# Attention product by two heads of both softmaxes with halves added on VectorE, and a unit stage whose order is written one instruction at a time

## The chip, the cores and the metric

The kernel runs on one core of a Trainium2 chip. The metric is the device time of one execution in microseconds (us). The core's engines each work through their own instructions in order: TensorE (PE in the profile; PEld is its loading of weights, which overlaps the matmuls), VectorE (DVE), ScalarE (ACT), GpSimd (POOL, here mostly an issuer of DMAs) and SyncE (SP, an issuer of DMAs).

## What is computed

A gated mix of two branches on the same 2048 x 1024 input, all in float32:

```python
g = sigmoid((x * gate_w).sum(-1, keepdims=True))
# branch a: linear attention, 32 heads of 32
q, k, v = split(x @ wqkv)
pq = einsum("bhsd,hdf->bhsf", q, w_phi);  pk = the same of k
phi_q = concat(softmax(pq), softmax(-pq));  phi_k = the same of pk
kv = einsum("bhsf,bhsd->bhfd", phi_k, v);  z = phi_k summed over s
o = (phi_q @ kv) / (phi_q . z + 1e-6)
a = o @ wo
# branch b: gated MLP, 3584 wide
b = (gelu(x @ w_gate) * (x @ w_up)) @ w_down
out = g * a + (1 - g) * b
```

## The kernel before

Every float32 product is made of three matmuls in `float32r`: an operand is split into a *high* part (a copy to `float32r` on ScalarE, L421) and a *low* part (operand minus high on VectorE, L424), and `PASSES` adds high-high, high-low and low-high. A weight tile so costs one ScalarE and one VectorE operation of 128x1024.

The program has three stages.

1. Keys, values, their feature maps, `kv`, `z` and the gate (L146 to L412). Query weights are folded with `w_phi` and stored in DRAM (`wq_fold`); `kv` and `z` go to DRAM as `kz`. VectorE sets `mask` and `ones` at the very start (L64 to L67, L149); `ones` feeds seven warm-up products of TensorE (L154), and `mask` makes the block-diagonal weights `bd` of the first folds.
2. The unit stage (L438 to L972): 62 *units*, each 2 of 28 column blocks of gate (`g`), up (`u`) or query (`q`) weights times half of the tokens, by Strassen's scheme (in Winograd's form). A unit is seven products of 12 matmuls (L744): `x` into bank `a`, `y` into bank `p`, `z` and `v` and so on, where the last two products of a unit stand inside the next one. `x`, `y`, `z` and `v` are the unit's weight operands, made from staged tiles by `weights` in the pools `wgu`, `tyz` and `v`. Between the products ScalarE copies one accumulating bank to another (`c<-b` L775, `c11<-a` L777, `b<-a` L779) and empties bank `p` (L757); `results` reads the finished banks, and gelu, the product with up, or the query itself goes out by DMA on GpSimd (`lm`, `q`). Bank `p` has a single buffer: the next unit's `y` product waits for L757.
3. The output stage (L975 to L1138): attention and MLP results times `wo` and `w_down`, 3024 matmuls (L1088).

Beside the units a *background* stream works on the queries. A *job* (`attention`, L838) is one block of 128 query features (4 heads) by 512 tokens, 32 jobs in all. It loads the block, transposes it 32 by 32, takes maximum and minimum, makes both softmaxes (ScalarE's exponent, with a table load), multiplies in the denominator and gate, transposes back, splits the result into `pts`, and hands TensorE an *attention product* (L906): for each of the two softmaxes three matmuls of 128x128 weights `kbs` and 512 columns, all into one bank `misc`. ScalarE copies the bank out (L909). The background also loads the second half's tokens between the jobs.

What sets the order: in the unit stage TensorE, VectorE, ScalarE and SyncE execute in the order in which the code is written (`manual_schedule`). That order comes from generators. Time is counted in *slots* of one product (t = 7n + k for product k of unit n). Each generator yields the earliest slot, the latest slot and the cost in VectorE and ScalarE time of its next piece of work; after each product, `run_slot` takes the pieces that are due and, as long as a budget of `SLOT` = 2.65 us on each of the two engines lasts, those that may run. An attention product is placed behind product 1 or 4 of a unit, at the earliest one slot after its operand `pts` was written.

Of the kernel before, what the change touches and what calls it, by code (L numbers as in the profile page):

```python
# [8 lines left out]
F32 = mybir.dt.float32  # L9
# [22 lines left out]
def tile_gated_mix(ctx: ExitStack, tc: tile.TileContext, x, xT, wkT, wqT, wv, w_phi, wo,  # L32
# [31 lines left out]
    mask = keep.tile([P, 4, 32], F32, name="mask")  # L64
    nc.vector.memset(mask, 0.0)
    for j in range(4):
        nc.vector.memset(mask[32 * j:32 * j + 32, j, :], 1.0)  # L67
# [78 lines left out]
    with tc.tile_pool(name="kw", bufs=1) as kw, tc.tile_pool(name="kp", bufs=1) as kp, \  # L146
            tc.manual_schedule(engines={PE, DVE}):
        ones = kp.tile([P, P], F32, name="ones")
# [89 lines left out]
        def finish_kv(hh, pkv):  # L238
# [10 lines left out]
            for h in range(4):  # L249
                q = h % 2  # L250
                nc.scalar.activation(kv_c[32 * h:32 * h + 32, 4 * hh:4 * hh + 4],
                                     by_head[32 * q:32 * q + 32, :, h // 2, :, q], AF.Copy)
            yield

        def finish_z(hh, s, zacc, pz):
            nc.tensor.matmul(pz, ones, zacc[:, s].rearrange("p h f -> p (h f)"), start=True, stop=True)
            z4 = pz.rearrange("p (g h f) -> p g h f", g=4, h=4)
            for h in range(4):
                q = slice(32 * h, 32 * h + 32)
                nc.scalar.activation(zb[q, 4 * hh:4 * hh + 4, s], z4[q, :, h, :], AF.Copy)  # L260
# [177 lines left out]
    with tc.tile_pool(name="xa", bufs=1) as xa, tc.tile_pool(name="fp", bufs=1) as fp, \  # L438
# [5 lines left out]
        SLOT, NEVER = 2.65, 10 ** 9  # L444
        streams, fillers, now, left = [], [], [0], [0.0, 0.0]

        def start(gen):
            streams.append([next(gen), len(streams), gen])

        def run_slot(t, extra=0.0, scalar=0.0):  # L450

            now[0] = t
            left[:] = [min(left[0], 0.0) + SLOT + extra, min(left[1], 0.0) + SLOT + extra - scalar]
            while True:
                ready = [s for s in streams if s[0][0] <= t and (s[0][1] <= t or (
                    left[0] > 0 and (left[1] > 0 or len(s[0]) < 4)))]
                if not ready:
                    break
                s = min(ready, key=lambda s: (s[0][1], s[1]))
                for i, cost in enumerate(s[0][2:]):  # L460
                    left[i] -= cost
                s[0] = next(s[2], None)
                if s[0] is None:
                    streams.remove(s)
# [3 lines left out]
        def room(n):  # L468

            return not any(held[max(0, len(held) - 4):][:max(0, n - 4 + min(4, len(held)))])  # L470

        def hold(*parts):
            held.append(True)
            return len(held) - 1, stage(*parts, pool=fp if len(held) % 4 == 0 else None)

        def hidden():
            return fp.tile([P, BLK], F32, tag="h", name="h", bufs=3)

# [15 lines left out]
        def late_sums(kc, r1, r2):  # L494
            x_load(1, kc, r1, r2)
            yield now[0] + 2, NEVER, 2.8
            for k, t in enumerate(x_sums(r1, r2)):
                nc.gpsimd.dma_start(xs_late[k][:, kc, :], t)
            yield now[0] + 2, NEVER, 0.0
# [6 lines left out]
        def second_half(t, staging):  # L506
# [7 lines left out]
            while not free[0]:  # L514
                yield now[0] + 1, NEVER, 0.0
# [3 lines left out]
            def load(n):  # L519
                i, j, _, _ = parts[n]  # L520
                nc.sync.dma_start(staging[n % 4].rearrange("p (a b) -> p a b", a=2), srcs[i][:, 2 * j:2 * j + 2, :])

            for n in range(4):
                load(n)
            for n, (i, j, last, need) in enumerate(parts):
                s = staging[n % 4].rearrange("p (a b) -> p a b", a=2)
                yield max(now[0], last), need - 2, 0.0, 1.05
# [5 lines left out]
                yield now[0], need - 1, 1.25  # L533
                low(q[1], s, q[0])
                if n + 4 < len(parts):
                    load(n + 4)
# [8 lines left out]
        right_ops = {}  # L545

        def weights(n, half, kind, m):
# [4 lines left out]
            yield t - 7, t - 6, 0.0  # L552
            while not room(2):
                yield now[0] + 1, t - 5, 0.0
            ke, e = hold((0, 1024, w[2 * m]))
            ko, o = hold((0, 1024, w[2 * m + 1] if fresh else right_sums[kind, m][0]))
            yield t - 5, t - 3, 0.0, 1.05
# [3 lines left out]
            yield now[0] + 1, t - 2, 1.25  # L561
            low(xl, e, xh)
            mine["x"] = x
            held[ke] = fresh
            yield max(now[0], t - 4), t - 2, 1.4 if fresh else 0.0, 1.05
            if fresh:
                b11, b21, b12, b22 = e[:, :BLK], e[:, BLK:], o[:, :BLK], o[:, BLK:]
                nc.vector.tensor_tensor(b22, b22, b12, OP.subtract)
                nc.vector.tensor_tensor(b12, b11, b12, OP.subtract)  # L569

# [5 lines left out]

            y = slot()
            yh, yl = flat(y)
            high(yh, o)
            if fresh:  # L580
                if half == 0:
                    nc.gpsimd.dma_start(right_sums[kind, m][0], o)
                if n:
                    yield now[0], t - 1, 1.4
                    more_sums()
            yield now[0] + 1, t, 1.25
            low(yl, o, yh)
            mine["y"] = y
            held[ko] = False
            if n == 0:  # L590
                yield now[0], t, 1.4
                more_sums()
            if not fresh:
# [580 lines left out]
```

## Time and profile before

| | us |
|---|---|
| median of 3 runs (2382.92 to 2386.14) | 2383.41 |
| the profiled execution, its own time | 2383.34 |
| its span, first to last instruction | 2381.5 |
| keys, values and gate, up to the first unit | 462.7 |
| unit stage, first unit product to first output product | 1228.3 |
| output stage, to the end of the span | 690.5 |

A row of a grouped view gives line, engine, operation, output and input tiles with partitions x elements and type, count, then busy time and mean nanoseconds of one, then the engine's idle time ahead of it and what ended it. A row of the timeline gives start, length, engine, line and count of merged instructions. A row of the waits gives who waited for whom, in total, how often, and the longest. PE matmul rows include the tail of the last matmul, which overlaps the next row's start.

### The profile page before, as it was taken

The page shows a single profiled execution, that of the slowest core. Times are in us where ns is not written, and L with a number is a line of the kernel's source. Part 1 is how long each engine was busy: PE and PEld are TensorE (multiplying, and loading weights), DVE is VectorE, ACT ScalarE, POOL GpSimd, SP SyncE. Part 2 cuts the span into 40 slices and gives each one's busy share as a digit, 9 for nine tenths or more (in the row PEclk, how much of TensorE's full clock was granted, in tenths as well). Part 3 has the DMA queues.
Part 4 walks back from the last instruction along what each step waited for, and adds up shares of the span by engine and source line. Part 5 has one row for each costly group of instructions (what it writes and reads, how often), then busy time and mean ns, then how long its engine had stood idle before and what let it go on. Part 6 is the DMA issues. An engine that isn't in the chain of part 4 may idle for free.

```text
span 2381.5 us, 28170 instructions
## 1 busy us (share of the span) xinstructions
PE 2372.2 (100%) x10689; PEld 1969.3 (83%) x10689; DVE 1746.3 (73%) x2183; ACT 991.6 (42%) x1286; POOL 142.2 (6%) x266
## 2 busy tenths in 40 slices
PE   9999999999999999999999999999999999999999
PEld 8888888788888888888888888888888888888887
DVE  7877868858777777777767676777574878777773
ACT  4323332435445444555555555555443222323221
POOL 0000000011111121110001000000000000000000
PEclk9999999999999999999999999999999999999999
DMA  5112333544444556474444444444685767978774
GB/s 179 47 47 84 98 115 100 180 174 146 179 170 149 194 199 229 171 254 140 138 133 158 142 134 133 153 138 135 240 292 182 252 223 264 327 260 316 261 267 135
DMA packets 154360, 425.10 MB, mean 179 GB/s; under 512 B 21360, under 2 KB 21360, under 8 KB 154224
## 3 DMA queue, kind: packets, MB, share of 16 engines
q1 hardware_dynamic: 127872, 336.64, 42.6%
q0 software_dynamic: 25312, 86.52, 9.4%
q8 instruction: 84, 1.38, 0.2%
q14 instruction: 52, 0.43, 0.1%
q10 hardware_dynamic: 1040, 0.13, 0.0%
HBM read 328.34 MB, written 94.90 MB: 178 GB/s over the span
## 4 chain that ended last, share of the span: by engine, by line
PE 79%; DVE 0%; ACT 0%; issue 0%; ACTq 0%; DVEq 0%
PE po L1088 29%; PE a L744 21%; PE c L744 14%; PE b L744 7%; PE p L744 7%; PE misc L906 2%; DVE x L1048 0%; ACT L872 0%; DVE x L888 0%; DVE tyz L424 0%; ACT x L872 0%; DVE st L876 0%; DVE x L879 0%; ACT tyz L421 0%; DVE v L424 0%
## 5 line engine op out<-in xcount | busy, mean ns | idle before, releaser
L200 PE MATMUL pd<-wkv,x 128*128 128x512 f32 x1536 | 361.3, 392 | 0.0
L200 PEld LDWEIGHTS pd<-wkv,x 128*128 128x128 f32 x1536 | 284.8, 188 | 58.1 <-issue 1.0
L1088 PE MATMUL po<-tw,wgu 128*128 128x512 f32 x1344 | 309.8, 389 | 0.0
L1088 PEld LDWEIGHTS po<-tw,wgu 128*128 128x128 f32 x1344 | 252.3, 188 | 52.4
L421 ACT ACTIVATE wgu<-stage 128x1024 fp32r<-128x1024 f32 x147 | 155.2, 1057 | 291.0 <-PE po L1088 225.1
L424 DVE TENSOR_TENSOR wgu<-stage,wgu 128x1024 fp32r<-128x1024 f32 x147 | 179.6, 1222 | 123.7 <-ACT wgu L421 123.5
L424 DVE TENSOR_TENSOR tyz<-stage,tyz 128x1024 fp32r<-128x1024 f32 x126 | 153.0, 1215 | 41.8 <-ACT tyz L421 41.8
L421 ACT ACTIVATE tyz<-stage 128x1024 fp32r<-128x1024 f32 x126 | 132.7, 1053 | 115.6 <-DVE stage L569 64.3
L744 PE MATMUL a<-s,tyz 128*128 128x512 f32 x744 | 179.4, 390 | 0.9 <-DVE tyz L424 0.4
L744 PE MATMUL a<-x,wgu 128*128 128x512 f32 x744 | 178.7, 389 | 0.0
L744 PE MATMUL p<-s,tyz 128*128 128x512 f32 x744 | 178.7, 389 | 0.0
L744 PE MATMUL c<-x,wgu 128*128 128x512 f32 x744 | 178.7, 389 | 0.0
L744 PE MATMUL b<-s,tyz 128*128 128x512 f32 x744 | 178.7, 389 | 0.0
L744 PE MATMUL c<-x,tyz 128*128 128x512 f32 x744 | 178.7, 389 | 0.0
L744 PE MATMUL a<-s,v 128*128 128x512 f32 x744 | 178.7, 389 | 0.0
L744 PEld LDWEIGHTS a<-s,tyz 128*128 128x128 f32 x744 | 139.4, 188 | 31.0 <-DVE tyz L424 1.3
L744 PEld LDWEIGHTS p<-s,tyz 128*128 128x128 f32 x744 | 139.6, 188 | 29.1
L744 PEld LDWEIGHTS a<-x,wgu 128*128 128x128 f32 x744 | 139.6, 188 | 29.0
L744 PEld LDWEIGHTS c<-x,tyz 128*128 128x128 f32 x744 | 139.6, 188 | 29.0
L744 PEld LDWEIGHTS c<-x,wgu 128*128 128x128 f32 x744 | 139.6, 188 | 29.0
L744 PEld LDWEIGHTS a<-s,v 128*128 128x128 f32 x744 | 139.6, 188 | 29.0
L744 PEld LDWEIGHTS b<-s,tyz 128*128 128x128 f32 x744 | 139.6, 188 | 29.0
(176 smaller groups left out, 3423.7 us busy)
## 6 DMA issues: line engine op xcount, KB each, us to landing
stage<-lm SPq DMA_DIRECT2D x98, 512.0 KB, 3.6
sr<-in_w_down SPq DMA_DIRECT2D x84, 512.0 KB, 5.8
sl<-lm SPq DMA_DIRECT2D x70, 512.0 KB, 4.5
lm<-h POOLq DMA_DIRECT2D x112, 256.0 KB, 2.5
stage<-in_w_gate SPq DMA_DIRECT2D x43, 512.0 KB, 3.9
stage<-in_w_up SPq DMA_DIRECT2D x43, 512.0 KB, 4.2
stage<-la SPq DMA_DIRECT2D x28, 512.0 KB, 4.3
tg<-stage POOLq DMA_DIRECT2D x26, 512.0 KB, 3.1
```

What stands on the lines that cost most here:

```text
L200: nc.tensor.matmul(ps[m], xb[b, kc // 4][:, a, kc % 4, t * P:(t + 1) * P], w[:, e, m * 512:(m + 1) * 512], start=kc == 0 and i == 0, stop= ...
L421: nc.scalar.activation(dst, src, AF.Copy)
L424: nc.vector.tensor_tensor(dst, src, dst_h.bitcast(F32), OP.subtract)
L744: nc.tensor.matmul(dst, w[:, h, 4 * part + kc, :], xq[:, e, kc, :], start=first and kc == 0 and i == 0, stop=kc == 3 and i == 2, skip_grou ...
L906: nc.tensor.matmul(po, kbs[:, a, s, :], pts[:, q, s, :], start=s == 0 and i == 0, stop=s == 1 and i == 2)
L1088: nc.tensor.matmul(ps[c], ls[:, a, m, c * P:(c + 1) * P], rs[:, e, m], start=opens and m == 0 and j == 0, stop=closes and m == 1 and j == 2)
```

## The change

Two things are changed together.

**The attention product.** The layout of a job becomes 2 heads x 2 softmaxes on the partitions: a block of 32 partitions holds one softmax of one head, and the tile's two halves of the free dimension hold two pairs of heads. So `load_query` loads each block twice (four DMAs of 32 partitions x 2 x 512 for one of 128x512), a signed copy on ScalarE (`sign`, plus and minus one by 32 partitions) turns the second copy negative, and one maximum does for both softmaxes. The block-diagonal weights of a pair are 64 columns wide instead of 128. Their high and low parts stand side by side in one 128x128 weight (`kbs`), so two matmuls (with `pts` high and `pts` low) do for a pair of heads what three did, with the low-low part in addition: 4 matmuls instead of 6, into two `misc` banks. The two halves of each result are then brought together: four half-height copies on ScalarE (`other` crosses partitions, `own` does not) and one addition on VectorE. `finish_kv` and `finish_z` write `kv_c` and `zb` in the new layout.

**The order.** The slots with budgets are replaced by estimated clocks of VectorE, ScalarE and TensorE. Each generator yields an engine, a length, the time from which the work can start, and a due product; `run` writes the requests one at a time by earliest start, then due, up to the estimated start of the next product. Constants stand for a product (2.73), a signal between engines, a DMA's landing (`LAND` = 5.0) and a store. Weight loads start up to nine products ahead of the unit, the bank copies and results are one sequence (`banks`), and an attention product goes behind any product whose estimated end is later than its operand. Query units stand at places 0, 5, 10 and 15 of the first half's 30 units instead of 2, 9, 16 and 23. `mask` moves to the first stage's pool, behind the new memsets.

```diff
-    mask = keep.tile([P, 4, 32], F32, name="mask")
-    nc.vector.memset(mask, 0.0)
+    pair_mask = keep.tile([P, 2, 32], F32, name="pair_mask")
+    nc.vector.memset(pair_mask, 0.0)
+    for j in range(2):
+        nc.vector.memset(pair_mask[64 * j:64 * j + 64, j, :], 1.0)
+    sign = keep.tile([P, 1], F32, name="sign")
     for j in range(4):
-        nc.vector.memset(mask[32 * j:32 * j + 32, j, :], 1.0)
+        nc.vector.memset(sign[32 * j:32 * j + 32], 1.0 - 2 * (j % 2))
...
-        SLOT, NEVER = 2.65, 10 ** 9
+        INF, PRODUCT, SIGNAL, LAND, STORE = 10.0 ** 9, 2.73, 0.12, 5.0, 4.5
...
+        def run(j, until):
             while True:
...
+                ready = []
+                for s in streams:
+                    at = max(busy.get(s[0][0], 0.0), value(s[0][2]))
+                    if at < until:
+                        ready.append((at, s[0][3], s))
+                if ready:
+                    at, due, s = min(ready, key=lambda r: r[:2])
...
+                emit(s)
...
-                mine.insert((0, 7, 12, 19)[m] if half else 7 * m + 2, (half, "q", m))
+                mine.insert((0, 7, 12, 19)[m] if half else 5 * m, (half, "q", m))
...
-            yield t - 5, t - 3, 0.0, 1.05
+            end = yield SCA, 1.1, lambda: max(landed, done(t - 9)), t - 2.2
             x = new_weight()
...
+                    yield SCA, 0.65, lambda: done(t + 1), t + 7.7
+                    nc.scalar.activation(before[2], unit_banks[n][1], AF.Copy)
...
+            product(*args, **kw)
+            ends[j] = begins[j] + PRODUCT
+            if fillers and fillers[0][0] < ends[j]:
+                fillers.pop(0)[1](ends[j] + 0.92)
...
-            nc.sync.dma_start(work[:, 4], query[half][g][j])
+            rows = query[half][g][j].rearrange("(w h f) t -> h f w t", w=2, h=2)
+            for h in range(2):
+                for s in range(2):
+                    nc.sync.dma_start(work[64 * h + 32 * s:64 * h + 32 * s + 32, 4:6], rows[h])
...
+                end = yield SCA, 1.1, landed, now[0] + SOON
+                nc.scalar.activation(e2, e2, AF.Copy, scale=sign)
...
-                nc.vector.transpose(work[:, 7], work[:, 4])
...
-                nc.vector.tensor_reduce(mm[:, 0, :], x, AX.X, OP.max)
-                nc.vector.tensor_reduce(mm[:, 1, :], x, AX.X, OP.min)
...
+                nc.vector.transpose(wide[1], wide[0])
...
+                nc.vector.tensor_reduce(mm, f, AX.X, OP.max)
...
+                for q in range(4):
+                    nc.vector.tensor_copy(k[32 * q:32 * q + 32], t[32 * (q ^ 1):32 * (q ^ 1) + 32])
...
-                        for i, (a, q) in enumerate(PASSES):
-                            nc.tensor.matmul(po, kbs[:, a, s, :], pts[:, q, s, :], start=s == 0 and i == 0,
-                                             stop=s == 1 and i == 2)
-                    h = hidden()
-                    nc.scalar.activation(h, po, AF.Copy)
...
+                po = [misc(), misc()]
+                for s in range(2):
+                    for q in range(2):
+                        nc.tensor.matmul(po[s], kbs[:, s].rearrange("p a b -> p (a b)"), pts[:, q, s, :],
+                                         start=q == 0, stop=q == 1)
...
+            for s in range(2):
+                nc.scalar.activation(other[rows[s]], po[s][rows[1 - s]], AF.Copy)
...
+            for s in range(2):
+                nc.scalar.activation(own[rows[s]], po[s][rows[s]], AF.Copy)
...
+            nc.vector.tensor_tensor(own, own, other, OP.add)
```

On VectorE, at the program's start (the rows are numbered by place in the engine's queue, with line, operation, output and input tiles and shape), before:

```order
1 L65 MEMSET mask 128x128
2 L149 MEMSET ones 128x128
3 L67 MEMSET mask 32x32 x4
4 L177 TENSOR_TENSOR bd<-phi_c,mask 128x128 x4
5 L44 TENSOR_TENSOR wkv<-early,wkv 128x512
```

And now:

```order
1 L65 MEMSET pair_mask 128x64
2 L70 MEMSET sign 32x1 x2
3 L67 MEMSET pair_mask 64x32 x2
4 L70 MEMSET sign 32x1 x2
5 L152 MEMSET mask 128x128
6 L154 MEMSET mask 32x32 x4
7 L156 MEMSET ones 128x128
8 L184 TENSOR_TENSOR bd<-phi_c,mask 128x128 x4
```

`ones`, on which TensorE's first instructions wait, was the second memset and is now the thirteenth.

On ScalarE, in the middle of the unit stage, around the copy that empties bank `p` of the first `u` unit (`x_3592<-p`, L757), before (`tyz` and `wgu` rows are highs of weights, L713 are gelus):

```order
220 L421 ACTIVATE tyz<-stage 128x1024
221 L779 ACTIVATE b<-a 128x512
222 L713 ACTIVATE x_3592<-x_3592 128x512
223 L421 ACTIVATE v<-stage 128x512
224 L757 ACTIVATE x_3592<-p 128x512
225 L775 ACTIVATE c<-b 128x512
226 L421 ACTIVATE tyz<-stage 128x1024
227 L777 ACTIVATE c_3590<-a 128x512
```

And the same place of the first `u` unit now (the copy from `p` is L830, the high is L428):

```order
235 L820 ACTIVATE b<-a 128x512
236 L428 ACTIVATE tyz<-stage 128x1024
237 L428 ACTIVATE v<-stage 128x512
238 L751 ACTIVATE x_3593<-x_3593 128x512
239 L428 ACTIVATE wgu<-stage 128x1024
240 L428 ACTIVATE tyz<-stage 128x1024
241 L830 ACTIVATE x_3593<-p 128x512
242 L809 ACTIVATE c<-b 128x512
```

The high of a later unit's `x` (row 239) and of the next unit's `z` (row 240) have moved ahead of the copy from `p`; they stood behind it, on the far side of `c<-b`.

On ScalarE, at the end of the unit stage (the last unit's bank `p`, the last copy `c<-b`, which TensorE's very last unit product needs, and the first weights of the output stage), before:

```order
1009 L421 ACTIVATE v<-stage 128x512
1010 L757 ACTIVATE x_3592<-p 128x512
1011 L807 ACTIVATE c<-b 128x512
1012 L421 ACTIVATE tyz<-stage 128x1024
1013 L421 ACTIVATE wgu<-stage 128x1024
1014 L421 ACTIVATE wl<-stage 128x1024
```

And now:

```order
1071 L751 ACTIVATE x_3593<-x_3593 128x512
1072 L830 ACTIVATE x_3593<-p 128x512
1073 L428 ACTIVATE tyz<-stage 128x1024
1074 L428 ACTIVATE wgu<-stage 128x1024
1075 L809 ACTIVATE c<-b 128x512
1076 L428 ACTIVATE wl<-stage 128x1024
```

The copy stood ahead of the two highs and stands behind them.

On TensorE, an attention product between unit products, before 6 matmuls and now 4; first before:

```order
262 L744 MATMUL a<-x_2482,wgu 128x512 x12
263 L744 MATMUL p<-s_3385,tyz 128x512 x12
264 L906 MATMUL misc<-pts,kbs 128x512 x6
265 L744 MATMUL c<-x_2287,tyz 128x512 x12
266 L744 MATMUL a<-s_3386,tyz 128x512 x12
```

And now:

```order
244 L793 MATMUL a<-s_3387,tyz 128x512 x12
245 L793 MATMUL a<-s_3389,v 128x512 x12
246 L995 MATMUL misc<-pts,kbs 128x512 x4
247 L793 MATMUL c_3591<-x_2682,wgu 128x512 x12
248 L793 MATMUL b<-s_3388,tyz 128x512 x12
```

There are 32 such places in both; the product now stands behind any of a unit's products and not only behind two of them.

More of the change, by code (lines that the diff above doesn't have):

```diff
@@ L891, in attention @@
[L891 removed]
+                end = yield VEC, 1.27, end - SIGNAL, now[0] + SOON
+                nc.vector.transpose(wide[1], wide[0])
+                more = bool(jobs) and stored.get(jobs[0], INF) < INF and not (
+                    between and now[0] >= between[0][0] - 7)
+                if more:
+                    landed = yield SYN, LAND, max(end, stored[jobs[0]]), INF
+                    load_query(*jobs[0])
+                end = yield SCA, 1.1, lambda: max(end, pts_free[0]), now[0] + SOON
```

492 lines of the change are left out of this document (272 added, 220 removed).

## The prediction

> **What bounds the kernel now.** I read the page first (busy shares, the row of the granted clock), then who made TensorE wait, then the stage that the change rewrites, then single places in order of time.
>
> ```profile
> PE 2372.2 (100%) x10689; PEld 1969.3 (83%) x10689; DVE 1746.3 (73%) x2183; ACT 991.6 (42%) x1286; POOL 142.2 (6%) x266
> PEclk9999999999999999999999999999999999999999
> ```
>
> TensorE is busy for 2372.2 of 2381.5 us and the clock is granted in full in every slice. So a shorter time needs fewer matmuls or fewer gaps between them, and of gaps there are only 9 us in all. The view of stretches gives the unit stage after its start-up and then its first half (columns: length, busy time of PE, PEld, DVE, ACT and POOL with their instructions, granted clock, DMA share, GB/s), and the view of waits names the only waits of TensorE in that stage:
>
> ```profile
> 473.00:1691.00 1218.00, 1217.58 (x5372) 1007.82 (x5371) 892.07 (x1194) 613.68 (x841) 132.17 (x244) 1.00 0.48 164
> 473.00:1070.00 597.00, 596.58 (x2633) 493.61 (x2632) 444.96 (x594) 286.74 (x395) 83.98 (x155) 1.00 0.53 186
> ```
>
> ```profile
> PE c L703 <- DVE h L651: 1.6, 1, 1.6
> PE a L744 <- DVE tyz L424: 0.4, 1, 0.4
> PE a L744 <- ACT c L777: 0.4, 1, 0.4
> ```
>
> TensorE stands still for 0.4 of 1218 us there. All three waits lie at the stage's first unit, where the order of the work is the same before and after. VectorE and ScalarE have 326 and 604 us to spare in the stage. The change can therefore win what it takes from TensorE's queue, and nothing on the other engines; it can lose whatever new waits it puts in that queue.
>
> **The term that is removed.** The timeline shows one attention product with the product behind it, and the grouped view all of them:
>
> ```profile
> 609.08 1.52 PE L906 MATMUL misc<-pts,kbs 128*128 128x512 f32 x6
> 610.44 2.88 PE L744 MATMUL c<-x,wgu 128*128 128x512 f32 x12
> 613.16 2.88 PE L744 MATMUL b<-s,tyz 128*128 128x512 f32 x12
> ```
>
> ```profile
> L906 PE MATMUL misc<-pts,kbs 128*128 128x512 f32 x192 | 48.7, 389 | 0.0
> ```
>
> A row's length counts the tail of its last matmul, which overlaps the next row, so the step from start to start is what counts: 610.44 - 609.08 = 1.36 us for six, 2.72 us for twelve, in both cases 0.2267 us a matmul. There are 192 / 6 = 32 attention products. Each goes from six matmuls to four of the same shape (128x128 weights, 512 columns), so 64 fewer: 64 x 0.2267 = **14.5 us off TensorE**. The 62 units keep their 7 products of 12 matmuls; they only stand in another sequence.
>
> **What is added elsewhere.** The nearest rows for a job's new work:
>
> ```profile
> L860 DVE STREAM_TRANSPOSE x<-x 128x512 f32<-128x512 f32 x32 | 22.6, 706 | 0.1
> L862 DVE TENSOR_REDUCE mm<-x 128x16 f32<-128x512 f32 x32 | 22.0, 686 | 1.1
> L863 DVE TENSOR_REDUCE mm<-x 128x16 f32<-128x512 f32 x32 | 21.7, 677 | 0.0
> L893 DVE STREAM_TRANSPOSE x<-x 128x1024 f32<-128x1024 f32 x32 | 39.6, 1238 | 0.0
> L880 DVE TENSOR_REDUCE st<-x 128x32 f32<-128x1024 f32 x32 | 39.1, 1220 | 1.1
> L721 DVE TENSOR_TENSOR h<-h,x 128x512 f32<-128x512 f32 x53 | 36.7, 692 | 1.8
> L406 DVE COPY g_at<-g_a 32x16 f32<-32x16 f32 x16 | 2.8, 173 | 0.2
> L909 ACT ACTIVATE h<-misc 128x512 f32<-128x512 f32 x32 | 19.2, 599 | 100.5 <-PE misc L906 100.5
> ```
>
> VectorE, per job: the first transpose is of 1024 instead of 512 (+0.53); one reduction of 1024 (1.22 by L880) replaces two of 512 (-0.14); four small copies (4 x 0.173 = 0.69, and not below 0.5, since the shortest memsets at the program's start take 0.12 each); the small operations double in width (about +0.1); the addition of the halves (+0.69). Together 1.9 us, 60 us in 32 jobs: VectorE goes from 892 to about 953 us in a stage of some 1204, 79%. ScalarE gets the signed copy (1.06, the longest of the highs of that size in the rows below) and four half-height copies for one full one; their cost by the row is 0.3 to 0.6 each, since no row shows whether half the partitions cost less; I take 0.6 by the nearest row, +1.8. That is at most 92 us, to 59%. Both lie beside TensorE, which hides them as long as no single operand comes late. Each job's one query load becomes four of 32 partitions, 512 KB instead of 256 KB, 8 MB in all; at 164 GB/s and a DMA share of 0.48 over the stage there is room. If the cover were gone, VectorE's 60 us would be the price; that is the third rival.
>
> **New waits, place by place.** The order on ScalarE in the middle of the stage shows the copy that empties bank `p` behind the highs of two weights, where it stood right behind the bank results before. TensorE's next `p` product waits for it. Its reserve, from the rows of the same work:
>
> ```profile
> 613.90 0.59 ACT L757 ACTIVATE x<-p 128x512 f32<-128x512 f32 x1
> 615.88 2.88 PE L744 MATMUL a<-x,wgu 128*128 128x512 f32 x12
> 616.08 0.58 ACT L775 ACTIVATE c<-b 128x512 f32<-128x512 f32 x1 [1.58 <-PE b L744]
> 617.96 1.04 ACT L421 ACTIVATE tyz<-stage 128x1024 fp32r<-128x1024 f32 x1
> 618.60 2.88 PE L744 MATMUL p<-s,tyz 128*128 128x512 f32 x12
> ```
>
> Before, the copy ends at 614.49 and `p` is written again at 618.60: 4.1 us in reserve. In the new order the high of `z` stands ahead of it, and that can start only when the `b` product has ended, 0.20 us behind the start of the `a` product (616.08 against 615.88). Then 1.06 for the high and 0.59 for the copy: 1.85 us, and the `p` product starts at 2.72. **0.87 us remain**, so no wait here, but the reserve is a fifth of what it was. The high of a weight (`tyz` or `wgu`) stands directly ahead of the copy in 9 of 62 units, so I count these as the places where a wait can come up, between 0 and 1 us each; I take 0.6 us in all, nearer to nothing, since the worked place still has room.
>
> At the stage's end the copy `c<-b` moves behind two highs:
>
> ```profile
> 1685.57 2.88 PE L744 MATMUL a<-s,v 128*128 128x512 f32 x12
> 1685.83 0.58 ACT L807 ACTIVATE c<-b 128x512 f32<-128x512 f32 x1 [1.46 <-PE b L744]
> 1688.29 2.88 PE L744 MATMUL c<-x,tyz 128*128 128x512 f32 x12
> 1689.03 1.06 ACT L421 ACTIVATE tyz<-stage 128x1024 fp32r<-128x1024 f32 x1 [2.62 <-DVE stage L928]
> 1690.00 1.04 ACT L421 ACTIVATE wgu<-stage 128x1024 fp32r<-128x1024 f32 x1
> ```
>
> Highs start 0.97 us apart (1690.00 - 1689.03). From 1685.83 two highs and the copy give 1685.83 + 1.94 + 0.58 = 1688.35, and the product that needs `c` would start at 1688.29. **+0.2 us** with the hand-over, once.
>
> At the program's start VectorE gets seven more memsets, and `ones` now stands behind all of them:
>
> ```profile
> 0.83 0.17 DVE L65 MEMSET mask<- 128x128 f32 x1 [0.83 <-PEq L1166]
> 0.97 0.17 DVE L149 MEMSET ones<- 128x128 f32 x1
> 1.08 0.47 DVE L67 MEMSET mask<- 32x32 f32 x4
> 1.19 3.36 PE L154 MATMUL pd<-ones 128*128 128x128 f32 x14 [1.19 <-DVE ones L149]
> 4.67 1.44 PE L190 MATMUL pg<-bd,early 128*128 128x128 f32 x8
> 6.98 0.58 ACT L43 ACTIVATE wkv<-pg 128x512 fp32r<-128x512 f32 x1
> 7.28 1.16 PE L190 MATMUL pg<-bd,early 128*128 128x128 f32 x8 [1.17 <-DMA early<-in_wkT]
> 8.19 1.64 PE L200 MATMUL pd<-wkv,x 128*128 128x512 f32 x6
> ```
>
> Eleven memsets at 0.11 to 0.14 stand between the first and `ones`: 1.3 us later, the warm-up matmuls end at about 5.9 instead of 4.6, and the first fold with them. The second fold waits for a DMA for 1.17 us anyway, so most of this is swallowed; the copy of the first fold's result can slip from 6.98 to about 7.5, and with it the product at 8.19. Between 0 and 0.5; I take **+0.3 us**.
>
> **The sum** against the profiled execution: its time was 2383.34 us (span 2381.5 and 1.8 around it), and the median of the runs is 2383.41, the same within 0.1. 2383.3 - 14.5 + 0.6 + 0.2 + 0.3 = 2369.9, say **2370 us**, 0.56% less.
>
> **The rivals.** *The waits are more and longer than worked out* (TensorE's new waits on `p` and on bank results in many units). For it: the reserves shrink, and ScalarE's and VectorE's orders are now packed. Against it: the places that I worked out have room, and the code lets an attention product into TensorE's order only behind a product that ends, by the code's clocks, after the operand is ready. If the nine places lose 1 us each, minus the 0.6 already counted, that is 2378; half of it 2374.
>
> *The query loads land late, and ScalarE stands still behind them: slower.* The signed copy waits for them in ScalarE's one queue, and the highs, the `p` copy and the bank copies behind it wait too. The issue view (KB each, median us to landing, over the unit stage):
>
> ```profile
> stage<-in_w_gate SPq DMA_DIRECT2D x39, 512.0 KB, 3.9
> x<-q SPq DMA_DIRECT2D x32, 256.0 KB, 2.7
> x<-xs SPq DMA_DIRECT2D x6, 512.0 KB, 6.0
> ```
>
> The order places the copy for a landing 5.0 us after the issue (`LAND`). Twice the bytes cost 1.2 us more (3.9 against 2.7), and three more issues at about 0.33 each add 1.0: 4.9 us, in time. By the slowest rows, 6.0 and 1.0 make 7.0, 2.0 us late. TensorE pays only what exceeds the reserve behind the copy: with 0.87 us that is 1.1 us in each job where a tight place follows. If it follows in 20 of 32 jobs, +22 us: 2392. It decides from 14.5 / 32 = 0.45 us of TensorE wait per job, that is, landings over 6.3 us at nearly every job. Against it: at the first job the reserve is larger, as `c` is wanted two products later. The Trainium skill, DMA: Bandwidth & Descriptors, section Rules for kernel authors, speaks against such a split: transfers to separate partition groups run through the same DMA engines one after the other, so one transfer over 128 partitions is to be used. By that page's fit (about 2.0 us and bytes over 436 GB/s, section Anatomy of one DMA — SWDGE (gpsimd) path, made for loads from GpSimd, so an estimate here) 512 KB in one go would land in 3.2 us and four in a row, each with its own 2.0 us, in over 9. The rows put a load of 256 KB at 2.7 us, near the page's 2.6, but no row here shows whether four loads in flight pay the fixed part four times; if they did, 4 us late less 0.9 in 20 jobs would be over 60 us, an estimate by the page alone.
>
> *VectorE becomes the bound where jobs crowd: no change.* Query units now stand at places 0, 5, 10 and 15 of the first 30 instead of 2, 9, 16 and 23, so the 16 jobs of the first half come in some 21 units. A job is about 12.4 us on VectorE: seven operations of 1024 at 1.22, three of 512 (2.07 by the rows above) and nine small ones of about 0.2. It becomes 14.3. The first half's row has 445 of 597 us; without 16 jobs at 12.4 that is 247, or 41%, for weights and results. In the 21 units, 420 us, 16 x 14.3 and 41% make 401 us. An in-order queue this full passes any delay on, and operands of TensorE stand in it. If it came out 3% longer, 12 us would build up, less about 3 us of reserve: 2370 + 9 = 2379. Against it: the code counts 1.25 us for operations that take 1.22 by the rows, and 0.72 to 0.75 for 0.69, so the real queue should run ahead of the one planned.
>
> *The change does not do what it says.* The order has 128 attention matmuls where it had 192, so it does.
>
> **How the numbers follow.** Forecast 0.70, at 2368.5 to 2372; more waits 0.16, at 2372 to 2378; a full VectorE 0.06, at 2379 (mostly within 0.2%); late loads 0.08, at 2380 to 2392. A measurement of this kernel tells 0.2%, about 4.8 us, from no change. Faster by more (below 2378.6): 0.70, nearly all of the second case and a little of the others, 0.87; within 0.2%: 0.07; slower by more (above 2388.2): 0.06. The range takes in the forecast and the second case, from 2367.8 (no new wait, 2368.8, and 1 us of the old start-up waits gone) to 2378.
>
> **What would show it.** Right: the group of `misc` matmuls with 128 entries and about 33 us, TensorE's waits in the unit stage below 2 us in all, the unit stage some 14 us shorter, the start of the unit stage within 0.5 us of where it was. Wrong: TensorE rows that wait on the copy from `p` or on `tyz`, ScalarE waiting on the query DMA, or VectorE busy near 100% for tens of microseconds in the stage's first third. A stage whose attention matmuls do not follow each other at 0.2267 us would fell the first term.

## The result and the profile after

The changed kernel takes **2370.73 us** (median of 4 runs, 2370.57 to 2371.59); the kernel before, on the same chip, takes 2384.24 us (4 runs, 2382.92 to 2386.14). The ratio is **0.9943**, with a 95% interval of 0.9926 to 0.9961: 13.5 us or 0.57% faster. The forecast was 2370.

First the busy shares of the changed kernel:

```profile
PE 2358.1 (100%) x10625; PEld 1957.5 (83%) x10625; DVE 1795.7 (76%) x2334; ACT 1078.7 (46%) x1388; POOL 142.2 (6%) x266
```

TensorE still fills the span, with 64 matmuls fewer (10625 for 10689); VectorE has 49.4 us more than before and ScalarE 87.1. The next view has the program in three stretches, start-up, unit stage and output stage (columns as in the prediction), first the kernel before, then the changed one:

```profile
0.00:462.69 462.69, 460.17 (x2263) 388.37 (x2264) 366.92 (x496) 165.83 (x219) 7.33 (x17) 1.00 0.33 104
462.69:1691.01 1228.32, 1225.86 (x5404) 1013.70 (x5403) 900.42 (x1205) 619.84 (x850) 133.79 (x247) 1.00 0.48 164
1691.01:2381.50 690.49, 686.13 (x3025) 567.22 (x3023) 478.98 (x483) 205.96 (x218) 1.08 (x2) 1.00 0.73 254
```

```profile
0.00:463.00 463.00, 459.67 (x2263) 388.15 (x2263) 367.42 (x503) 164.42 (x211) 7.33 (x17) 1.00 0.32 104
463.00:1677.86 1214.86, 1212.80 (x5340) 1001.92 (x5339) 951.70 (x1352) 708.23 (x960) 133.76 (x247) 1.00 0.51 173
1677.86:2368.80 690.94, 685.60 (x3025) 567.38 (x3023) 476.59 (x481) 206.04 (x217) 1.08 (x2) 1.00 0.74 254
```

The unit stage is 13.46 us shorter, the start-up 0.31 and the output stage 0.45 us longer; together the 12.7 us by which the spans differ (2381.5 and 2368.8). In the unit stage VectorE works 51.3 us more and ScalarE 88.4. TensorE's waits in the changed kernel, all that there are:

```profile
PE pd L161 <- DVE ones L156: 2.5, 1, 2.5
PE c L740 <- DVE h L689: 1.6, 1, 1.6
PE pg L197 <- DMA early<-in_wkT: 0.8, 1, 0.8
PE a L793 <- ACT c L813: 0.4, 1, 0.4
```

Two of them lie in the unit stage, both at its first unit, where they were before. No new wait came up. The attention product in order of time, and its group:

```profile
529.12 2.89 PE L793 MATMUL a<-s,v 128*128 128x512 f32 x12
531.84 1.10 PE L995 MATMUL misc<-pts,kbs 128*128 128x512 f32 x4
532.78 2.89 PE L793 MATMUL c<-x,wgu 128*128 128x512 f32 x12
```

```profile
L995 PE MATMUL misc<-pts,kbs 128*128 128x512 f32 x128 | 35.2, 397 | 0.0
```

From start to start the four take 532.78 - 531.84 = 0.94 us, where four times 0.2267 is 0.907. With the old step of 1.36, 32 x (1.36 - 0.94) = 13.44 us. Added up over all 32 places the steps take 43.5 us before and 30.2 now, 13.3 less: all but 0.2 us of the unit stage's gain. (The wait of 0.4 us on `tyz` at the first unit is gone as well; the stage's end, next, takes 0.16 of it back.) The stage's end, on TensorE and then on ScalarE:

```profile
1672.26 2.88 PE L793 MATMUL a<-s,v 128*128 128x512 f32 x12
1675.01 3.02 PE L793 MATMUL c<-x,tyz 128*128 128x512 f32 x12
1677.86 11.04 PE L1190 MATMUL po<-tyz,wgu 128*128 128x512 f32 x48
```

```profile
1672.45 1.06 ACT L428 ACTIVATE tyz<-stage 128x1024 fp32r<-128x1024 f32 x1 [1.40 <-PE b L793]
1673.42 1.05 ACT L428 ACTIVATE wgu<-stage 128x1024 fp32r<-128x1024 f32 x1
1674.37 0.58 ACT L809 ACTIVATE c<-b 128x512 f32<-128x512 f32 x1
```

The copy `c<-b` stands behind the two highs as foreseen and ends at 1674.95; the `c` product starts at 1675.01. The last two products take 5.60 us instead of 2 x 2.72: +0.16.

The new work on VectorE and ScalarE, and the issue view of the query loads (KB each, median us to landing):

```profile
L963 DVE COPY st<-st 32x32 f32<-32x32 f32 x128 | 22.1, 173 | 2.4
L1015 DVE TENSOR_TENSOR h<-h,other 128x512 f32<-128x512 f32 x32 | 21.9, 686 | 5.0 <-ACT h L1012 4.9
L1006 ACT ACTIVATE other<-misc 64x512 f32<-64x512 f32 x64 | 38.1, 595 | 43.8 <-PE misc L995 43.1
L924 ACT ACTIVATE x<-x,sign 128x1024 f32<-128x1024 f32 x32 | 36.7, 1148 | 18.2 <-DMA x<-q 11.5 <-DMA kz<-kz 4.2 <-DMA stage<-in_w_up 2.3
x<-q SPq DMA_DIRECT2D x128, 128.0 KB, 2.7
```

### The profile page after: what moved, and what is told of

Its sections match the earlier page's. It is cut to its first block, busy times and chain, and to the rows that moved or that the text cites. A ratio compares the mean times of both kernels' runs of the same rounds, so it can differ in the third digit from the quotient of the medians.

```text
span 2368.8 us, 28503 instructions
## 1 busy us (share of the span) xinstructions
PE 2358.1 (100%) x10625; PEld 1957.5 (83%) x10625; DVE 1795.7 (76%) x2334; ACT 1078.7 (46%) x1388; POOL 142.2 (6%) x266
## 3 DMA queue, kind: packets, MB, share of 16 engines
q8 instruction: 83, 1.36, 0.2%
## 4 chain that ended last, share of the span: by engine, by line
PE 88%; issue 9%; DVE 1%; DMA 1%; ACT 0%; POOL 0%; SPq 0%; POOLq 0%; ACTq 0%
PE po L1190 29%; PE a L793 21%; PE c L793 14%; PE pd L207 7%; PE b L793 7%; PE p L793 7%; PE misc L995 1%; PE pg L241 1%; PE pd L197 0%; DMA raw<-in_xT 0%; PE pg L197 0%; DMA early<-in_wkT 0%; POOL wq L293 0%; DMA stage<-in_wqT 0%; DVE x L1150 0%
## 5 line engine op out<-in xcount | busy, mean ns | idle before, releaser
L428 ACT ACTIVATE wgu<-stage 128x1024 fp32r<-128x1024 f32 x147 | 155.8, 1060 | 295.6 <-PE po L1190 224.3
L793 PEld LDWEIGHTS a<-s,tyz 128*128 128x128 f32 x744 | 139.5, 188 | 30.2 <-ACT c L813 0.8
L428 ACT ACTIVATE tyz<-stage 128x1024 fp32r<-128x1024 f32 x126 | 132.9, 1055 | 54.2 <-PE c L793 18.1
```

The source lines that it names most:

```text
L428: nc.scalar.activation(dst, src, AF.Copy)
L793: nc.tensor.matmul(dst, w[:, h, 4 * part + kc, :], xq[:, e, kc, :], start=first and kc == 0 and i == 0, stop=kc == 3 and i == 2, skip_grou ...
```

## The experiments

All diffs are against the changed kernel unless the text says otherwise. Where the text says "one run", there is a single time, and a difference of a microsecond between two such times shows little.

### Six matmuls in the new order

```diff
-                    for q in range(2):
+                    for i, q in enumerate((0, 1, 1)):
                         nc.tensor.matmul(po[s], kbs[:, s].rearrange("p a b -> p (a b)"), pts[:, q, s, :],
-                                         start=q == 0, stop=q == 1)
+                                         start=i == 0, stop=i == 2)
```

> The changed kernel in its new order, but each attention product again with six matmuls (the second p-stack is multiplied twice, so the attention output is not the reference's). Theory (the gain is the 64 matmuls taken off TensorE's queue, the new order by itself is worth nothing): unit stage longer by 64 x 0.2267 = 14.5 us than in the changed kernel, about 2385 us, within 0.2% of the time before; attention steps 1.36 to 1.40 us. Rival (part of the gain comes from the new order): below 2379 us with a unit stage well under 1228 us. Second rival (the added work on VectorE and ScalarE costs time that the missing matmuls hid): above 2388 us.

Measured: 2384.95 us (median of 10) against 2383.28 of the kernel before (13 runs on the same chip), a ratio of 1.0006, 0.9996 to 1.0015. The theory holds: with the matmuls put back the whole gain is gone, and neither the new order nor the 51 and 88 us of added work gains or costs anything that this measurement can tell. The attention step here:

```profile
531.38 1.56 PE L995 MATMUL misc<-pts,kbs 128*128 128x512 f32 x6
532.78 2.89 PE L793 MATMUL c<-x,wgu 128*128 128x512 f32 x12
```

1.40 us for six where the kernel before took 1.36: the 0.04 us of slowing per attention product is there with six matmuls as with four.

### The new product in the old order

The kernel before with the new layout, product and `joined` addition as a stream of its own; slots, budgets and the order's rules as before:

```diff
-                run_slot(7 * n + k, 1.0 if fill else 0.0, 0.6 * (moved + fill))
+                run_slot(7 * n + k, 0.9 if fill else 0.0, 0.6 * (moved + 4 * fill))
...
+        def joined(own, other, half, g, j):
+            yield now[0] + 2, now[0] + 3, 0.7
+            nc.vector.tensor_tensor(own, own, other, OP.add)
+            spill(own, left_att[half], j, g)
```

> The new attention product (two heads by two softmaxes, four matmuls, VectorE adds the halves) inside the old slot-by-slot order of the unit stage, with the query units at their old places. Theory (count of matmuls alone): unit stage shorter by about 13.5 us than before, 2370 to 2373 us. Rival (the new work fits beside TensorE only in an order written instruction by instruction): new TensorE waits on bank copies, p or results of together over 4 us, 2375 us or more.

Measured: 2477.01 us (median of 4), a ratio of 1.0392, 1.0375 to 1.0409. The theory falls, and the time is on the rival's side, far beyond its number. Its mechanism, waits on bank copies and results, is only a small part of it: the one such wait of note takes 4.1 us, on the copy from `p`. TensorE's largest wait, and the last attention products in order of time:

```profile
PE misc L921 <- ACT pts L428: 83.9, 5, 17.6
```

```profile
1697.34 0.79 PE L921 MATMUL misc<-pts,kbs 128*128 128x512 f32 x1 [13.71 <-ACT pts L428]
1717.86 0.80 PE L921 MATMUL misc<-pts,kbs 128*128 128x512 f32 x1 [17.61 <-ACT pts L428]
```

The slots give a job only what the weights and results leave. With 1.6 us more per job the jobs fall behind, and five of the 32 are left when the last product of the stage has run. They then go one after the other with TensorE standing still, about 20.5 us each (1717.86 - 1697.34). The waits are hardly spread over the stage; this is a backlog paid at the end.

### Old order, with room for the jobs

The kernel of the run before this one with two edits:

```diff
-        SLOT, NEVER = 2.65, 10 ** 9
+        SLOT, NEVER = 2.96, 10 ** 9
...
-                mine.insert((0, 7, 12, 19)[m] if half else 7 * m + 2, (half, "q", m))
+                mine.insert((0, 7, 12, 19)[m] if half else 5 * m + 1, (half, "q", m))
```

At these places the four query units stand between a gate unit and its up unit and write over a kept gate result, so four pairs of the MLP come out of other numbers; the instructions are the same in number and size.

> The new attention product in the old slot-by-slot order as in e2_product_old_order, with the query units of the first half moved ahead (places 1, 6, 11, 16 instead of 2, 9, 16, 23) and 2.96 instead of 2.65 us of VectorE and ScalarE work let into a slot, so that by the code all 32 attention products stand ahead of the stage's last product. Theory (what the old order lacked in e2 was room for the jobs, so five were left over behind the last product; TensorE's count decides once they fit): attention steps of 0.91 us, unit stage 1214 to 1220 us, 2369 to 2377 us. Rival (slots that are fuller than TensorE's 2.72 us make TensorE wait for weights and banks in many units; an order written instruction by instruction is needed): unit stage over 1225 us, 2381 us or more.

Measured: 2383.94 us (median of 10) against 2384.12, a ratio of 1.000, 0.999 to 1.001. The backlog is gone, but so is the gain; the time lies just over the rival's bound. The two largest waits of TensorE in its unit stage:

```profile
PE b L751 <- ACT b L786: 5.5, 1, 5.5
PE a L751 <- DVE tyz L431: 2.5, 3, 1.6
```

These two make 8.0 us, and what runs behind a wait is slower as well (below). So in slots that can be filled this far the product's gain is given back in waits. Its attention matmuls, though, take the old 389 ns in the mean, not 397, with the same two banks and the same four matmuls:

```profile
L921 PE MATMUL misc<-pts,kbs 128*128 128x512 f32 x128 | 34.2, 389 | 0.0
```

### The start-up

```diff
+        ones = kp.tile([P, P], F32, name="ones")
+        nc.vector.memset(ones, 1.0)
...
-    nc.vector.memset(pair_mask, 0.0)
```

(the memsets of `pair_mask` and `sign` follow once the start-up's own are done.)

> The changed kernel with the memset of the ones tile put first on VectorE and the memsets of pair_mask and sign moved behind the start-up. Theory (the later start of the unit stage, 463.00 instead of 462.69 us, comes from the later warm-up matmuls): unit stage starts at 462.6 to 462.8 us, time 0.2 to 0.4 us less than the changed kernel. Rival (it comes from something else in the start-up): start stays at 463.0 us.

Measured, one run: 2371.32 us, and the warm-up matmuls did start early:

```profile
1.05 3.35 PE L156 MATMUL pd<-ones 128*128 128x128 f32 x14 [1.05 <-DVE ones L147]
```

The first row of the unit stage in this run, and then the warm-up and the first row of the unit stage in the run with the new product in the old order, whose memsets stand as in the changed kernel:

```profile
463.03 2.88 PE L793 MATMUL a<-x,wgu 128*128 128x512 f32 x12
```

```profile
2.49 3.34 PE L161 MATMUL pd<-ones 128*128 128x128 f32 x14 [2.49 <-DVE ones L156]
462.34 2.88 PE L751 MATMUL a<-x,wgu 128*128 128x512 f32 x12
```

The theory falls: with an early warm-up the stage starts late, with a late one early. Over the runs of this study whose start-up is the changed kernel's own, the stage starts between 462.33 us (three reductions more on VectorE, below) and 463.30 (eight loads, below); what decides within this microsecond was not settled.

### One bank for the four matmuls

```diff
-                po = [misc(), misc()]
+                po = [misc()] * 2
...
-                                         start=q == 0, stop=q == 1)
+                                         start=s == 0 and q == 0, stop=s == 1 and q == 1)
```

> The changed kernel with all four attention matmuls of a job accumulated into one bank instead of two into each of two banks (the halves of two softmax pairs are added up where they should stand apart, so the output is not the reference's). In the changed kernel four matmuls take 0.94 us from start to start of the products around them, 0.033 us more than 4 x 0.2267. Theory A (the extra comes from the second bank, its start and its signal): the step falls to 0.907 us and the unit stage is 1.0 us shorter. Theory B (it comes from the operands, the waits or the signals of the matmuls themselves): the step stays at 0.94 us.

Measured, one run: 2371.87 us; the row of the attention matmuls' group is the same as the changed kernel's above, 35.2 us and 397 ns.

Theory A falls: the second bank is not the cause. With the two runs above, the 0.03 to 0.04 us go with the written order and not with the number of matmuls or of banks. What in that order does it stays open; it is worth 1.1 us in all.

### Later query loads

The four loads of a job cut into eight or sixteen:

```diff
-                    nc.sync.dma_start(work[64 * h + 32 * s:64 * h + 32 * s + 32, 4:6], rows[h])
+                    for i in range(0, 32, 8):
+                        p = 64 * h + 32 * s + i
+                        nc.sync.dma_start(work[p:p + 8, 4:6], rows[h][i:i + 8])
```

> The changed kernel with each job's query load of four transfers of 32 partitions cut into sixteen of 8 partitions (32 KB each). By the issue view of the changed kernel the four land in 2.7 us each; sixteen issues at some 0.33 us put the last landing about 8 us behind the first issue. Theory (late loads make ScalarE wait, TensorE pays only what exceeds its reserve, as the second rival of the prediction had it): the signed copy waits 3 to 4 us in most jobs and TensorE some 1 to 2.5 us in up to 20 jobs, 2375 to 2420 us. Rival A (the place of the copy in ScalarE's queue lies later than the code's clocks say): ScalarE waits more, TensorE's new waits stay under 2 us, 2371 to 2373 us. Rival B (by the Trainium skill, DMA: Bandwidth & Descriptors, section Rules for kernel authors, that transfers to separate partition groups run one after the other): the fixed part of each is paid sixteen times, the last lands over 20 us behind the first issue, and the time is above 2430 us.

> The changed kernel with each job's query load cut into eight transfers of 16 partitions. In e8_sixteen_loads the sixteen issues took 5.4 us and the last landed about 7.8 us behind the first issue; eight should take 2.7 us and land after some 5.2 us, at the 5.0 us that the written order reckons with. Theory (TensorE pays only for landings beyond the reserve, and the point lies near 6 us): within 4 us of the changed kernel, 2370 to 2375 us. Rival (each extra issue on SP costs by itself, in proportion, a third of the 53 us of sixteen): 2385 us or more.

Measured, one run each: sixteen loads 2423.71 us, 53.0 more than the changed kernel; eight loads 2380.44, 9.7 more. One job's issues on SP, first in the changed kernel, then with eight, then with sixteen:

```profile
621.49 1.74 SPq L906 DMA_DIRECT2D x<-q  x4
```

```profile
622.55 3.59 SPq L908 DMA_DIRECT2D x<-q  x8
```

```profile
627.61 5.43 SPq L908 DMA_DIRECT2D x<-q  x16
```

With eight, a load lands 2.2 us after its own issue in the median, where it was 2.7 with four (issue view):

```profile
x<-q SPq DMA_DIRECT2D x256, 64.0 KB, 2.2
```

So the loads run beside each other, and what comes late is their issue: the last of a job's data is there some 1.7 + 2.7 = 4.4 and 3.6 + 2.2 = 5.8 us behind the first issue. For sixteen the view gives no landing; with 2.2 to 2.7 us it would be 7.6 to 8.1, an estimate. The signed copy, which needs all sixteen, starts 8.6 us behind the first issue in the median and 11.8 at the latest. The time rises by 0, 9.7 and 53.0 us, so by these single runs the bend lies between 4.4 us and 5.8. By the prediction's working it lies at 5.0 + 0.87 = 5.9, and 14.5 us would be paid at 6.3. ScalarE's signed copy waits 100.3 us with sixteen, in 24 of the 32 jobs, where it waited 18.2:

```profile
L926 ACT ACTIVATE x<-x,sign 128x1024 f32<-128x1024 f32 x32 | 36.7, 1148 | 100.3 <-DMA kz<-kz 50.3 <-DMA x<-q 30.6 <-DMA stage<-in_w_gate 19.5
```

```profile
PE p L793 <- ACT x L830: 14.3, 9, 3.9
PE a L793 <- ACT c L813: 8.9, 5, 3.5
PE a L793 <- DVE h L769: 6.4, 2, 6.1
PE b L793 <- ACT b L820: 5.7, 2, 5.5
```

The first row puts most of the wait on loads of `kz` and of weights, but the signed copy reads neither; where it waits, it starts 2.6 us in the median behind its job's last query issue, about the time of a landing. The second fence holds TensorE's waits of the same run: three of the four name ScalarE copies that stand behind the signed copy. The four make 35.3 us; the slowing behind the long ones (last section) adds to them. The theory's mechanism holds, its upper end of 2420 was a little low. Rival A falls, and so does rival B, the Trainium skill's rule in DMA: Bandwidth & Descriptors, section Rules for kernel authors, taken as the full fixed part for each load. For eight loads neither theory's number was met: the cost is 9.7 us, between 4 and a third of 53, and 5.9 of it fell at a single place, in a wait of 4.2 us on VectorE (`h`, L769) and the slowed product behind it.

### Work that the order does not know of

In the changed kernel, extra copies of 128x1024 on ScalarE, behind the signed copy in each job (two, then one), or extra max reductions of 1024 columns on VectorE (three, then one); in the kernel before, three extra sum reductions of 1024:

```diff
+                for _ in range(2):
+                    nc.scalar.activation(e2, e2, AF.Copy)
...
+                nc.vector.tensor_reduce(mm, f, AX.X, OP.max)
```

> The changed kernel with two more copies of 128x1024 on ScalarE in each attention job (in place, values unchanged): 2 x 1.05 us, 67 us more on ScalarE in all, which the written order does not know of. Theory (ScalarE is covered by TensorE but the reserve behind the signed copy is 0.9 us, as the prediction had it): TensorE waits on ScalarE in jobs where a tight place follows, up to 1.2 us in some 20 of 32 jobs, 2372 to 2395 us. Rival (the real queue runs far enough ahead of the written one): no new wait of TensorE over 1 us in all, within 1 us of the changed kernel.

> The changed kernel with one extra copy of 128x1024 on ScalarE per job: 1.05 us per job, 34 us in all, half of e6_act_extra, which cost 22 us. Theory (reserve of about 0.9 us behind the signed copy, as the prediction worked out): under 4 us, 2370 to 2375 us. Rival (in proportion, no reserve): 11 us, 2380 us or more.

> The changed kernel with the max reduction of each attention job done four times instead of once: 3 x 1.22 us, 117 us more on VectorE, about 1066 of 1205 us in the unit stage (88%), without the written order knowing of it. Theory (VectorE's added 60 us of the change are hidden with room to spare): less than 12 us of new TensorE waits, below 2383 us. Rival (VectorE is already close to being the bound, the third rival of the prediction): TensorE waits on VectorE of tens of us, 2395 us or more.

> The changed kernel with the max reduction of each job done twice: 1.22 us more on VectorE per job, 39 us in all, a third of e7_dve_extra, which cost 58.6 us. Theory (there is a reserve per job, and only what exceeds it is paid): under 5 us, below 2376 us. Rival (no reserve, half of every microsecond of work that the order does not know is paid): some 20 us, 2385 to 2395 us.

> The kernel before with its sum reduction of each job done four times: 3 x 1.22 us more on VectorE per job, 117 us in all, the same as in e7_dve_extra. Theory (the change used up reserve: the old order had more room on VectorE, 892 of 1218 us): less is paid than the 58.6 us of e7, under 30 us, below 2414 us. Rival (the slot order has no more room): 2440 us or more.

Measured, one run each:

| run | added work, by the row of one | time | more than its base |
|---|---|---|---|
| after, one copy on ScalarE | 34 us | 2373.74 | 3.0 |
| after, two copies on ScalarE | 67 us | 2392.80 | 22.1 |
| after, one reduction on VectorE | 39 us | 2374.71 | 4.0 |
| after, three reductions on VectorE | 117 us | 2429.30 | 58.6 |
| before, three reductions on VectorE | 117 us | 2460.81 | 76.3 (on 2384.56) |

On either engine the first microsecond per job is nearly free and what lies beyond is paid, as the theory of a reserve had it. But for three reductions the theory "hidden with room to spare" falls: half of the 117 us comes through. The rival's time was reached, its reason only in part: VectorE is busy for 1064 of the stage's 1275 us and not full, and TensorE's waits come to 27 us on ScalarE and 13 on VectorE, spread over the stage. The largest rows, and then the wait of ScalarE's exponent on VectorE in the changed kernel and in this run:

```profile
PE b L793 <- ACT b L820: 13.8, 7, 4.5
PE p L793 <- ACT x L830: 9.8, 11, 1.5
PE a L793 <- DVE x L761: 6.8, 6, 2.4
```

```profile
ACT L940 <- DVE x L938: 13.5, 9, 3.9
ACT L943 <- DVE x L941: 88.5, 21, 7.6
```

The last row of the table speaks against my view that the change had used up reserve: the same work costs the kernel before 76.3 us though its VectorE was 51 us emptier. The written order has less slack at single places and yet took this unplanned work better than the slots did, with one run of each and with the reductions at different places of the job (maximum after, sum before). The rival's side won here, by its own bound of 2440.

No run here beats the changed kernel.

## Why the prediction was right

**The term that is removed** was right in kind, and the run with six matmuls ties the gain to it: in the new order they take the time of the kernel before. Its size was 14.5, and 13.3 to 13.4 came out. The step that was off is "in both cases 0.2267 us a matmul" carried over to the new order: there the product takes 0.94 us, not 0.907, which is 32 x 0.033 = 1.1 us less gain.

**The waits on the `p` copy** (0.6) did not come: no wait on it stands in the rows of the changed kernel. The reserve of 0.87 us held: the tightest places, four of them, have 0.97 to 0.98 us left, each behind a high of `tyz`, as here:

```profile
519.40 0.58 ACT L830 ACTIVATE x<-p 128x512 f32<-128x512 f32 x1
520.96 2.43 PE L793 MATMUL p<-s,tyz 128*128 128x512 f32 x10
```

`p` is, though, the bank that waits most when the loads come late (14.3 us with sixteen).

**The stage's end** (+0.2) came out at +0.16 by just the chain given: two highs, the copy, the product.

**The start-up** (+0.3) came out at +0.31, but not shown to be for the reason given. With `ones` first again the unit stage did not start earlier, and with `ones` late it started at 462.34 in another run. The term was right by chance, within a scatter three times its size. The output stage's +0.45, which the prediction did not have, is within scatter too: over the runs with the changed kernel's output stage it takes 689.8 to 691.0 us. With the 0.6 that did not come and the 1.1 that went missing, the misses cancel in part (1.1 + 0.45 - 0.6, about 0.9 us): 2369.9 forecast, 2370.73 measured.

**The added work** was reckoned at 60 us for VectorE and at most 92 for ScalarE; the unit stage has 51.3 and 88.4 more. A small copy takes 173 ns and the addition of the halves 686, as taken. A half-height copy takes 595 ns, the upper end of its bound. "Both lie beside TensorE" held, but the study shows on what it hangs: in the old order the same work makes the kernel 94 us slower than before, or, with room for the jobs, takes the whole gain. The prediction argued from busy shares and from single places; that the order had to be rewritten for this cover it did not say, and it is the main thing that it left out.

**The rivals.** Late loads: ScalarE does wait on query loads in the changed kernel, 11.5 us in all, and TensorE pays nothing; at 2.7 us a landing the loads are in time. The last landing came at 4.4 us where 4.9 was reckoned. The mechanism is real, and with eight and sixteen loads its bend lies close to the place given. "Over 60 us" by the Trainium skill's rule, for four loads, did not come, nor did the rule hold for sixteen when read as one full fixed part after the other. VectorE as the bound: one reduction more, 39 us or 4% of its work in the stage, costs 4.0 us, where the prediction reckoned 9 for 3%. More waits: none.

## What to carry to other kernels

A matmul off a full TensorE queue was worth its step here, no more, and only if the work that replaces it on other engines fits into their order. Busy shares of 73 and 42% did not tell this: against the written order the same work cost 13 us in the slots with room and 106 us in the slots as they were. Before such a trade, add the planned work alone to the kernel (an idempotent reduction repeated, say) and see what comes through; and look for a backlog, which shows as one stretch of the span with an idle TensorE, not as a longer wait everywhere.

## What the runs showed of the hardware

A wait costs TensorE more than its length. A product of twelve takes 2.88 us by its row. Behind a short wait it takes 3.01 to 3.06 (3.33 to 3.37 at the first unit); behind waits of 2.5 us and more it took 4.3 to 5.5 in 12 of 13 places of these runs, at a lower granted clock, and between 1.7 and 2.5 us both came up. One short wait (the old order with room), then two long ones and the stretch behind each (sixteen loads; the granted clock is the third number from the end):

```profile
697.49 3.01 PE L751 MATMUL p<-s,tyz 128*128 128x512 f32 x12 [0.44 <-ACT x L764]
```

```profile
808.84 4.52 PE L793 MATMUL p<-s,tyz 128*128 128x512 f32 x12 [3.90 <-ACT x L830]
1446.17 5.49 PE L793 MATMUL a<-x,wgu 128*128 128x512 f32 x12 [6.13 <-DVE h L769]
```

```profile
808.84:810.84 2.00, 2.00 (x7) 1.62 (x8) 2.00 (x4) 1.99 (x4) 0.00 (x0) 0.79 0.54 217
1446.17:1448.17 2.00, 2.00 (x5) 1.61 (x6) 2.00 (x4) 1.95 (x5) 0.54 (x1) 0.50 0.78 252
```

And the kernel before with three extra reductions, behind a wait of 1.91 us:

```profile
1345.87 4.61 PE L744 MATMUL a<-x,wgu 128*128 128x512 f32 x12 [1.91 <-DVE h L719]
```

So 1.4 to 2.6 us are lost behind such a wait on top of it, and a prediction that prices waits at their length is too low once they are long. The Trainium skill, TensorE: Matmul & The Clock Gate, section Part 1: The HAM clock gate, states that the clock falls to half after an idle window of about 3.4 us. The halved clock agrees (0.50 in the last row of the stretches); but a wait of 1.91 us was already enough here to slow the product, at a granted clock of 0.57 in the 2 us behind it, while one of 1.92 us in the same run and one of 3.47 us with sixteen loads were not.

Copies from a bank of 64 partitions take as long as of 128 (595 ns by L1006, 599 before by the row in the prediction), and four loads of 128 KB issued together land in 2.7 us each, as one of 256 KB did; eight of 64 KB land in 2.2.
